# The second phase of a routed expert kernel in a written-out TensorE order

## The chip, the cores and the metric

One core of a Trainium2 chip runs the whole program. The metric is device time in microseconds (us), the median of three runs. Engines: PE is TensorE (matrix products and transposes), DVE is VectorE, ACT is ScalarE, POOL is GpSimd, SP is SyncE, which issues most transfers.

## The reference

The reference computes attention with a threshold, then a dense layer whose hidden value is the largest of three products, then one expert out of eight for each of the 2304 tokens (512 wide, experts 1024 wide):

```python
logits = x @ w_gate + modality_bias[modality_id]
e_idx = np.argmax(logits, axis=1)
...
for e in range(E):
    mask = e_idx == e
    h = np.maximum(x[mask] @ w1[e], 0.0)
    out[mask] = gate_w[mask, None] * (h @ w2[e])
```

Here `x` is the output of the dense layer, and `gate_w` the softmax value of the chosen expert.

## The kernel before

**Arithmetic.** Most products work on operands that are split into a rounded part and the rest (`xh`, `xl`, `wh`, `wl`); one product of the reference is three products on PE, and a `split_out` (ACT rounds, DVE subtracts) stands ahead of each.

**First phase** (`phase1`, `run_tiles`). Attention goes over 128-row tiles: scores (L244), maximum and mask (L259, L254), exponential (L281), transposes (L299, L300), products with the values (L352, in `av`). The dense layer, `moe1`, works on blocks of 256 tokens, nine in all (0 to 8). It is a generator: it issues a few products (L415 for the hidden values, L444 for the output) and yields the time that they stand for, and `fill` runs it between the tiles of attention. A hidden group is 24 products into one PSUM bank; DVE takes maxima from it (L425), ACT rounds (L429), POOL subtracts (L430). Block 6's output, blocks 7 and 8 are left over when attention ends.

**Second phase** (`phase2`). A token's logits (`logits`, `last_logits`: transpose, product with the gate weights, add the bias) lead to the routing. `route_part` finds each token's expert and its place among the tokens of that expert; two small products (L805, L806) count across partitions. `early` does this when blocks 0 to 7 have logits, takes the expert with the most tokens (`estar`), and makes the *early slot*: 384 of its tokens that can be worked on before block 8's tokens are known. `final` does it for all tokens and lays out the other slots of 384 tokens with one expert each; five of them are static. `invert` turns "token goes to place" into "place holds token" by one product for each 128 tokens with the matrix `r_loh` (L860): first the token numbers (`tok`, `gidx`), then a second set for `gate` and `sidx`. A slot is worked through so: POOL gathers its tokens from `xd` in DRAM by `gidx` (L1027), `tokens` transposes and splits them (L1041, `x2h`, `x2l`, 3 sets of 128), `up` makes 8 hidden tiles (12 products of 384 columns each, L1074), `down` adds 72 products of 512 columns (L1095) into three banks, ACT scales them by `gate` (L1099), and POOL scatters the three results to `out` by `sidx` (L1100). `weights` loads and splits an expert's weights, eight pieces of 128x1024, two pieces ahead (L1052, L1054, L1055).

**What sets the order.** The program's text gives a first order, and a planner then moves each engine's instructions by priority and modelled readiness: any PE product may go ahead of an earlier one that is held up. `hot` raises the priority of the routing; `issue_after` holds some work behind an instruction. The order of the end of routing and the early slot stands in `phase2` itself (L560 to L606). Banks: `psM` has two, shared by `moe1`, attention's values and the inversions; in the second phase `moe1` takes `psM` and the two `ph2` banks in turn; three `y2p` and one `pt2` (token transposes) are the rest. Every scatter writes the tensor `out`, so each waits for the one before.

Of the kernel before, what the change touches and what calls it, by code (L numbers as in the profile page):

```python
# [22 lines left out]
E, F2 = 8, 1024  # L23
# [25 lines left out]
class Kern:  # L49
# [5 lines left out]
    def open(self, stack, name, bufs, space=None, side="left"):  # L55
        kw = dict(side=side, reuse_waits="tile")
        if space is not None:
            kw["space"] = space
        return stack.enter_context(self.tc.tile_pool(name=name, bufs=bufs, **kw))

# [177 lines left out]
    def scores(self, lhs):  # L238

        nc = self.nc  # L240
        ps = self.psS.tile([128, 2, 512], F32, name="s")
        for hh in range(2):
            for i, (st, kk) in enumerate(lhs):
                nc.tensor.matmul(ps[:, hh, :288], lhsT=st, rhs=kk[:, hh * 288:hh * 288 + 288],  # L244
                                 start=i == 0, stop=i == len(lhs) - 1)
        return ps
# [47 lines left out]
    def transposes(self, p, outs, p4, c4):  # L294
# [3 lines left out]
        for kt in range(4):  # L298
            nc.tensor.transpose(pt[:, kt, :], p[:, kt * 128:kt * 128 + 128], self.idn)  # L299
        nc.tensor.transpose(p4[:, c4:c4 + 128], p[:, 512:], self.idn)  # L300
# [31 lines left out]
    def av(self, hd, xf):  # L332
# [3 lines left out]
        if hd["na"]:  # L336
# [4 lines left out]
            for kt in range(KT):  # L341
                kk = 128 if kt < 4 else 64
                nc.tensor.matmul(ps[js, :nq], lhsT=f32(hd["vv"][:kk, kt, 0, :]), rhs=f32(hd["pt"][0][:kk, kt, :nq]),  # L343
                                 start=kt == 0, stop=kt == 4)
# [4 lines left out]
        for kt in range(KT):  # L349

            for i, t in enumerate(hd["pt"][:2 if kt < 4 else 1]):
                nc.tensor.matmul(ps[:, :nq], lhsT=vv[:, kt, :, :].rearrange("p a d -> p (a d)"),  # L352
# [48 lines left out]
    def moe1(self, i):  # L401
# [4 lines left out]
        for n0 in range(0, 3 * KF, 2):  # L406
            ps = self.psA()
            for s in range(2):
# [5 lines left out]
                for n, (a, r) in enumerate(ops):  # L414
                    nc.tensor.matmul(ps[:, s * BLK:s * BLK + BLK], lhsT=a, rhs=r, start=n == 0, stop=n == len(ops) - 1)  # L415
                    if n % 4 == 3 and (n < 11 or s == 0):
                        yield 440
            for s in range(2):
# [7 lines left out]
                if m == 2:  # L426
# [5 lines left out]
                    hL.append(l)  # L432
            yield 440
        x1s = []
        for t in range(2):
# [7 lines left out]
            for n, (a, r) in enumerate(ops):  # L443
                nc.tensor.matmul(ps, lhsT=a, rhs=r, start=n == 0, stop=n == len(ops) - 1)  # L444
# [9 lines left out]
        self.x1s = x1s  # L454

    def logits(self, i, x1s):
        nc = self.nc
        for t in range(2):
# [3 lines left out]
            for kc in range(KD):  # L462
                nc.tensor.transpose(pt[:, kc, :], x1[:, kc * 128:kc * 128 + 128], self.idn)
            x1t = self.po.tile([128, KD, 128], F32, name="x1t", bufs=1)
            nc.vector.tensor_copy(x1t, pt)
            yield 440
            pl = self.psL()[:, 0, :]
            for kc in range(KD):
                nc.tensor.matmul(pl[:, :E], lhsT=x1t[:, kc, :], rhs=self.wgs[:, kc, :], start=kc == 0, stop=kc == KD - 1)
            nc.vector.tensor_tensor(self.lg[:, tt, :], pl[:, :E], self.bias[:, tt, :], op=ALU.add)  # L470
            yield 440
        self.logged = i + 1

    def last_logits(self):
        nc = self.nc
        i = NBLK - 1
        xt = []
        for t in range(2):
            pt = self.psL()
            for kc in range(KD):  # L480
                nc.tensor.transpose(pt[:, kc, :], self.x1s[t][:, kc * 128:kc * 128 + 128], self.idn)
# [5 lines left out]
        yield  # L487
        pl = self.psL()
        for t in range(2):
            for kc in range(KD):  # L490
                ins = nc.tensor.matmul(pl[:, t, :E], lhsT=xt[t][:, kc, :], rhs=self.wgs[:, kc, :], start=kc == 0, stop=kc == KD - 1)
        nc.vector.tensor_tensor(self.lg[:, 2 * i:2 * i + 2, :], pl[:, :2, :E], self.bias[:, 2 * i:2 * i + 2, :], op=ALU.add)
        yield ins.ins
# [41 lines left out]
    def phase2(self):  # L535
# [6 lines left out]
        self.nacc = 0  # L542

        def acc():
            self.nacc += 1
            if self.nacc % 2 == 0:
                return self.psM.tile([128, 512], F32, name="m")
            return self.ps2.tile([128, 512], F32, name="ph2", bufs=2)

        self.psA = acc  # L550
        self.route_tiles()
        parts = [self.route_part(0, 14), self.early()]
        need = [14 // 2, 16 // 2]
        self.sidegap = self.tailgap
        while self.fillers or self.side or parts:
            while parts and self.logged >= need[0]:
                self.side.append(parts.pop(0))
                need.pop(0)
            self.fill(1.0)
        t0 = self.eslot  # L560
        hot = lambda: tc.high_priority(offset=self.hot)
        with hot():
            lg = self.last_logits()
            next(lg)
        self.up(t0, 1, (0,))
        with hot():
            ins = next(lg)
        self.p1.close()
        self.pb = opn(ctx, "p2b", 1)
        fin = self.final()  # L570
        with tc.issue_after(ins):
            self.up(t0, 1, (1,))
        with hot():
            ins = next(fin)
        with tc.issue_after(ins):
            self.up(t0, 2)
            self.up(t0, 3)
            self.down(t0, 0)
            self.down(t0, 1)
        with hot():  # L580
            ins = next(fin)
        with tc.issue_after(ins):
            self.down(t0, 2)
        with hot():
            for _ in fin:
                pass
        last = self.estar
        for t in range(NSTAT):
            c = slice(t * G3, t * G3 + G3)
            e = nc.sync.value_load(self.eT[0:1, t * G3:t * G3 + 1], min_val=0, max_val=E - 1)  # L590
            self.slots.append(self.new_slot(self.pa if t % 2 else self.pb, e, e != last, self.gidx[:, c], self.sidx[:, c], self.gate[:, c]))
            last = e
        for t, sl in enumerate(self.slots):
            nxt = self.slots[t + 1] if t < NSTAT else None
            if nxt:
                self.gather(nxt, G3)
            for c in range(NC):
                if t:
                    self.up(sl, c)
                if t and c and nxt:  # L600
                    self.tokens(nxt, c - 1)
            for c in range(NC):
                if t or c > 2:
                    self.down(sl, c)
                if t == 0 and c:
                    self.tokens(nxt, c - 1)  # L606
        n = nc.values_load(self.eT[0:1, NTL:], min_val=NSTAT * G3, max_val=NTL)  # L607
        with tc.For_i(NSTAT * G3, n, G3) as i:
# [9 lines left out]
            sl = self.new_slot(self.pa, e, None, ix[:, :G3], ix[:, G3:], gt)  # L618
# [4 lines left out]
            for c in range(NC):  # L623
                self.up(sl, c)
            for c in range(NC):
                self.down(sl, c)
# [73 lines left out]
    x1s = None  # L700
    conv_rate = (1, 1)
    conv_credit = 0
    tailgap = 3
# [76 lines left out]
    def route_part(self, i0, i1):  # L780
# [23 lines left out]
        pw = self.psM.tile([128, 512], F32, name="m")  # L804
        nc.tensor.matmul(pw[:, :n * E], lhsT=self.below, rhs=ohf, start=True, stop=True)  # L805
        ins = nc.tensor.matmul(pw[:, 256:256 + n * E], lhsT=self.ones, rhs=ohf, start=True, stop=True)  # L806
        self.pw_ins = ins.ins
        ex = t(G, "ex")
        nc.scalar.activation(ex, sh, AF.Exp)
        yield 200  # L810
# [15 lines left out]
        yield 0  # L826
# [11 lines left out]
        yield 0  # L838

    def invert(self, tl, i1, n, name):  # L840
# [12 lines left out]
        for k0, k1 in ((0, 2), (2, NK)):  # L853
# [3 lines left out]
                              self.vals[:, :, k0:k1][:, :i1].rearrange("p t (k o) -> p t k o", o=1).to_broadcast(full), op=ALU.mult)  # L857
            p = self.psM.tile([128, 512], F32, name="m")[:, :(k1 - k0) * n]
            for i in range(i1):
                ins = nc.tensor.matmul(p, lhsT=self.loh[:, i, :], rhs=R[:, i].rearrange("p k s -> p (k s)"),  # L860
                                       start=i == 0, stop=i == i1 - 1)
            tok = t([128, k1 - k0, n], f"tok{k0}")
            v.tensor_copy(tok, p.rearrange("p (k s) -> p k s", s=n))  # L863
            if k0 == 0:
                sc = t([128, n], "sc")
# [291 lines left out]
```

## Time and profile before

| | before |
|---|---|
| median of 3 runs | 931.27 us (930.74 to 932.67) |
| the profiled execution | 935.56 us |
| its span, first to last instruction | 933.8 us |
| mean granted PE clock | 0.966 |
| busy PE / DVE / ACT / POOL | 873.1 / 627.1 / 561.9 / 441.6 us |

The profile is of one execution, whose span is 1.8 us shorter than its time; the median of the runs is 4.3 us below that time. Attention ends at about 609 us, block 8 begins at 645.6 us, the early slot at 687.9, the first static slot at 746.9, and PE's last product starts before 920.9. A product's duration holds its way through the array; what a stream of them costs is the distance between their starts.

### The profile page before, as it was taken

The page shows a single profiled execution, that of the slowest core. Times are in us where ns is not written, and L with a number is a line of the kernel's source. Part 1 is how long each engine was busy: PE and PEld are TensorE (multiplying, and loading weights), DVE is VectorE, ACT ScalarE, POOL GpSimd, SP SyncE. Part 2 cuts the span into 40 slices and gives each one's busy share as a digit, 9 for nine tenths or more (in the row PEclk, how much of TensorE's full clock was granted, in tenths as well). Part 3 has the DMA queues.
Part 4 walks back from the last instruction along what each step waited for, and adds up shares of the span by engine and source line. Part 5 has one row for each costly group of instructions (what it writes and reads, how often), then busy time and mean ns, then how long its engine had stood idle before and what let it go on. Part 6 is the DMA issues. An engine that isn't in the chain of part 4 may idle for free. (4 is left out here: it accounts for less than half of the span.)

```text
span 933.8 us, 16780 instructions
## 1 busy us (share of the span) xinstructions
PE 873.1 (93%) x5598; PEld 775.6 (83%) x5598; DVE 627.1 (67%) x1589; ACT 561.9 (60%) x1167; POOL 441.6 (47%) x635
## 2 busy tenths in 40 slices
PE   7877999999999999999989999999789899999994
PEld 4545876778799899999889999899778698899893
DVE  6998997645588787998797889552525634534430
ACT  4777876756688878889887888611222434444430
POOL 4777877554566667857676765211200212021001
PEclk9998999999999989999989999999789999999998
DMA  6555453322322322322322221000500223411000
GB/s 178 157 160 144 129 150 87 109 63 59 93 57 58 97 71 67 107 67 62 95 77 73 75 69 31 12 13 23 214 2 24 61 64 132 128 57 46 1 34 36
DMA packets 58234, 74.26 MB, mean 80 GB/s; under 512 B 27424, under 2 KB 40480, under 8 KB 58144
## 3 DMA queue, kind: packets, MB, share of 16 engines
q1 hardware_dynamic: 54448, 63.66, 23.5%
q0 software_dynamic: 2880, 9.44, 2.9%
q8 instruction: 46, 0.75, 0.3%
q14 instruction: 44, 0.36, 0.1%
q10 hardware_dynamic: 816, 0.04, 0.1%
HBM read 80.46 MB, written 9.44 MB: 96 GB/s over the span
## 5 line engine op out<-in xcount | busy, mean ns | idle before, releaser
L415 PE MATMUL m<-xh,w 128*128 128x256 f32 x1152 | 235.6, 294 | 4.0 <-DVE e_tok L863 2.2
L415 PEld LDWEIGHTS m<-xh,w 128*128 128x128 f32 x1152 | 190.6, 196 | 7.6 <-DVE e_tok L863 2.4
L415 PE MATMUL m<-xl,w 128*128 128x256 f32 x576 | 167.0, 290 | 1.1 <-POOL xl L379 1.1
L254 DVE SCALAR_TENSOR_TENSOR e<-s,mx,e 128x576 f32<-128x576 f32 x144 | 116.8, 812 | 26.7 <-ACT e L281 23.5
L259 DVE TENSOR_REDUCE mx<-s 128x1 f32<-128x576 f32 x144 | 106.6, 748 | 38.5 <-PE s L244 37.6
L281 ACT ACTIVATE e<-s,mx 128x576 f32<-128x576 f32 x144 | 106.9, 743 | 22.5 <-DVE mx L259 15.5
L415 PEld LDWEIGHTS m<-xl,w 128*128 128x128 f32 x576 | 113.2, 197 | 1.8 <-POOL xl L379 1.3
L1074 PE MATMUL ph<-x2h,w 128*128 128x384 f32 x384 | 107.3, 352 | 1.4 <-ACT x2h L285 1.4
L244 PE MATMUL s<-kk,qh 128*128 128x288 f32 (+1 forms) x272 | 89.5, 359 | 12.4 <-DVE e L254 6.6
L1095 PE MATMUL y2p<-w 128*128 128x512 f32 x432 | 100.8, 391 | 0.0
L216 POOL TENSOR_TENSOR kk<-kr,kk 64x576 fp32r<-64x576 f32 x60 | 88.0, 1467 | 17.7 <-ACT kk L215 8.2
L299 PE MATMUL pt<-idn,e 128*128 128x128 f32 x576 | 91.5, 282 | 4.4 <-ACT th L309 2.6
L1095 PEld LDWEIGHTS y2p<-w 128*128 128x128 f32 x432 | 80.6, 188 | 16.3
L1078 DVE SCALAR_TENSOR_TENSOR w<-ph,w 128x384 fp32r<-128x384 f32 x48 | 26.7, 555 | 90.7 <-ACT w L1077 90.6
L739 DVE TENSOR_TENSOR tl<-pc,th 128x512 fp32r<-128x512 f32 (+1 forms) x104 | 78.3, 760 | 9.7 <-ACT th L311 9.2
L299 PEld LDWEIGHTS pt<-idn,e 128*128 128x128 f32 x576 | 70.5, 145 | 12.2 <-ACT th L309 3.9
L430 POOL TENSOR_TENSOR hl<-hacc,hh 128x256 fp32r<-128x256 f32 x54 | 42.0, 777 | 81.3 <-ACT hh L429 76.8
L267 POOL COPY e<-mx 128x64 f32<-128x64 f32 x144 | 48.6, 342 | 65.8 <-DVE mx L266 51.7
L1077 ACT ACTIVATE w<-ph 128x384 fp32r<-128x384 f32 x48 | 23.6, 492 | 85.7 <-PE ph L1074 84.3
L1074 PEld LDWEIGHTS ph<-x2h,w 128*128 128x128 f32 x384 | 72.8, 195 | 2.6 <-ACT x2h L285 2.1
L343 PE MATMUL m<-th,vv 128*64 128x256 f32 (+3 forms) x240 | 69.1, 427 | 4.2 <-ACT th L322 2.2
L244 PEld LDWEIGHTS s<-kk,qh 128*128 128x128 f32 (+1 forms) x272 | 54.2, 202 | 22.4 <-issue 9.4
(225 smaller groups left out, 2034.0 us busy)
## 6 DMA issues: line engine op xcount, KB each, us to landing
r<-w SPq DMA_DIRECT2D x48, 512.0 KB
kr<-k SPq DMA_DIRECT2D x120, 144.0 KB
tl<-w SPq DMA_DIRECT2D x18, 512.0 KB
qr<-q SPq DMA_DIRECT2D x120, 64.0 KB
vr<-v SPq DMA_DIRECT2D x40, 160.0 KB
xd<-x SPq DMA_DIRECT2D x18, 256.0 KB
vv<-v SPq DMA_DIRECT2D x24, 160.0 KB
tl<-wo SPq DMA_DIRECT2D x6, 512.0 KB
```

What stands on the lines that cost most here:

```text
L216: nc.gpsimd.tensor_tensor(kk[64:128], kr[64:128], f32(kk[64:128]), op=ALU.subtract)
L244: nc.tensor.matmul(ps[:, hh, :288], lhsT=st, rhs=kk[:, hh * 288:hh * 288 + 288], start=i == 0, stop=i == len(lhs) - 1)
L254: self.conv_step(v.scalar_tensor_tensor(e, sv, mx[:, 1:2], e, op0=ALU.is_ge, op1=ALU.mult, accum_out=mx[:, 2:3]))
L259: self.conv_step(v.tensor_reduce(mn[:, 0:1], sn, axis=AX.XY, op=ALU.max, negate=True))
L267: nc.gpsimd.tensor_copy(cur[3][:, S:], mx[:, 4:5].to_broadcast([128, 64]))
L281: nc.scalar.activation(e, sv, AF.Exp, bias=mx[:, 0:1], scale=1.0)
L299: nc.tensor.transpose(pt[:, kt, :], p[:, kt * 128:kt * 128 + 128], self.idn)
L343: nc.tensor.matmul(ps[js, :nq], lhsT=f32(hd["vv"][:kk, kt, 0, :]), rhs=f32(hd["pt"][0][:kk, kt, :nq]), start=kt == 0, stop=kt == 4)
L415: nc.tensor.matmul(ps[:, s * BLK:s * BLK + BLK], lhsT=a, rhs=r, start=n == 0, stop=n == len(ops) - 1)
L739: nc.vector.tensor_tensor(l, src, f32(h), op=ALU.subtract)
L1074: nc.tensor.matmul(ph, lhsT=w[:, cs], rhs=x[:, kc, :], start=n == 0, stop=n == 3 * KD - 1)
L1095: nc.tensor.matmul(sl["y"][g], lhsT=a, rhs=r[:, i, :], start=f == 0 and n == 0, stop=f == KF2 - 1 and n == 2)
```

## The change

- From the end of attention on (`pinned`), every PE product and transpose keeps the order of the program (`mm`, `tp`); the planner no longer moves them, nor past attention's earlier products.
- That order is made by `drive`: a `main` generator (what is left of `moe1`, then slot after slot) yields the time of what it has issued, and side work (logits, `early`, `late_routing`, the next slot's tokens) is put in when the time that it asked for has passed, one piece after the other.
- The early slot is worked as a whole after block 8, beside the end of routing; before, two of its hidden tiles stood ahead of block 8's last groups. Its eight weights are loaded and split during block 8. Its tokens are transposed between products of block 8.
- `invert` for the first static slot is done alone (`g`, 3 places of 39) and its gather issued; then `experts` makes the expert table for slots, not for places; then the inversion of all (`f`).
- `moe1` takes three `ph2` banks in turn, and the token transposes take `psM`.
- The scatters write `dram_disjoint_views` of `out`, one for each set, which are taken as not overlapping.

```diff
+    def mm(self, *args, **kw):
+        return self.pin(self.nc.tensor.matmul(*args, **kw))
...
@@ moe1
+            if i == NBLK - 1 and self.eslot and n0 >= 6:
+                self.weights(n0 // 2)
             yield 440
...
@@ phase2
-        self.psA = acc
+        self.psA = lambda: self.ps2.tile([128, 512], F32, name="ph2", bufs=3)
+        self.outs = dram_disjoint_views(self.out, (NSTAT + 2) * G3)
...
+        self.pinned = True
+        self.slots = []
+        parts = [(lambda: self.logged >= 7, self.route_part(0, 14)), (lambda: self.logged >= 8, self.early()),
+                 (lambda: self.x1i == NBLK - 1, self.late_routing())]
+        self.drive(self.main(), parts)
...
+    def drive(self, main, parts):
+        t = 0.0
+        cur, at = None, 0.0
+        for ns in main:
+            forced = ns is None
+            t += ns or 0.0
+            while True:
+                if cur is None:
+                    if self.side:
+                        cur = self.side.pop(0)
+                    elif parts and parts[0][0]():
+                        cur = parts.pop(0)[1]
+                    else:
+                        break
+                    at = t
+                if t < at and not forced:
+                    break
+                forced = False
+                try:
+                    at = max(t, at) + next(cur)
+                except StopIteration:
+                    cur = None
...
+        for t in range(NSTAT + 1):
+            while len(self.slots) <= t or len(self.slots[t]["done"]) < G3:
+                yield None
+            sl = self.slots[t]
+            if 1 < t < NSTAT:
+                self.side.append(self.next_tokens(self.slots[t + 1]))
+            yield from self.slot(sl)
...
@@ early
+        inv = self.invert(tl, i1, G3, "e", 5000)
+        yield next(inv)
         sc, gidx, _ = next(inv)
...
+        self.gather(sl, G3)
...
         for g in range(G3):
+            yield 3500 if g else 6500
+            self.tokens(sl, g)
...
@@ final
+        first = self.invert(tl, NTT, G3, "g", 10000, rest=False)
+        yield next(first)
+        _, gidx, ins = next(first)
+        with self.tc.issue_after(ins.ins):
+            ins = self.experts(t, nt, st, n1)
+        with self.tc.issue_after(ins.ins):
+            inverse = self.invert(tl, NTT, NTL, "f", 6000)
+            wait = next(inverse)
...
+        self.gather(sl, G3)
+        for g in range(G3):
+            yield 3500 if g else 5000
+            self.tokens(sl, g)
...
@@ tokens
-        pt = self.ps2.tile([128, 4, 128], F32, name="pt2", bufs=1)
+        pt = self.psM.tile([128, 512], F32, name="m").rearrange("p (a b) -> p a b", b=128)
...
@@ down
-                nc.gpsimd.indirect_dma_start(out=self.out, out_offset=bass.IndirectOffsetOnAxis(ap=sl["sidx"][:, g:g + 1], axis=0),
+                nc.gpsimd.indirect_dma_start(out=sl["out"][g], out_offset=bass.IndirectOffsetOnAxis(ap=sl["sidx"][:, g:g + 1], axis=0),
```

What this does to the order, at three places. All PE products of the changed kernel have the lines of `mm` and `tp` (L69, L72).

First PE at the end of attention, before: behind the last transposes (`pt`) stand products of block 6 (`m`, `ph` from `w`), and attention's last values product (`vv`) comes after 20 of them.

```order
L300 MATMUL p_8538<-idn,e 128x128
L299 MATMUL pt<-idn,e 128x128 x4
L444 MATMUL m<-w,hl 128x512
L444 MATMUL m<-w,hh 128x512
L444 MATMUL ph_8646<-w,hh 128x512
...
L444 MATMUL ph_8646<-w,hh 128x512
L463 MATMUL y2p<-idn,x_8643 128x128 x2
L352 MATMUL m<-th,vv 128x320
```

The same place now:

```order
L72 MATMUL pt<-idn,e 128x128 x4
L72 MATMUL p_8538<-idn,e 128x128
L69 MATMUL m<-th,vv 128x320
L69 MATMUL m<-tl,vv 128x320
...
L69 MATMUL m<-th,vv 128x320
L69 MATMUL m<-w,hh 128x512 x2
L69 MATMUL m<-w,hl 128x512
```

The values product now stands right behind the transposes that it needs, and block 6's products behind it.

Second PE at the early slot's tokens (`xg`), before: three sets in a row between block 8 and the slot's first hidden tile.

```order
L444 MATMUL m<-w,hh 128x512
L1041 MATMUL pt_9344<-idn,xg 128x128 x4
L1041 MATMUL pt_9366<-idn,xg 128x128 x4
L1041 MATMUL pt_9386<-idn,xg 128x128 x4
L1074 MATMUL ph_9416<-x2h,w 128x384
```

Now, the first two of the three:

```order
L69 MATMUL ph_9482<-xh,w 128x256 x2
L72 MATMUL m<-idn,xg 128x128 x4
L69 MATMUL ph_9482<-xl,w 128x256
...
L69 MATMUL ph_9528<-xh,w 128x256
L72 MATMUL m<-idn,xg 128x128 x4
L69 MATMUL ph_9571<-w,hh 128x512
```

Each set now stands between products of block 8 (`ph_9482`, `ph_9528`, `ph_9571`); the third stands between `ph_9571` and `ph_9601`.

Third DVE at the early slot's index, before (`e_tok` is what the inversion gives, L1055 the split of a weight):

```order
L863 COPY e_tok_9287<-m 128x6
L866 SCALAR_TENSOR_TENSOR e_sc<-e_tok_9287 128x3
L868 CAST e_gidx<-e_sc 128x3
L1055 TENSOR_TENSOR w<-r_8614,w 128x1024 x3
L863 COPY e_tok_9321<-m 128x12
```

Now:

```order
L874 COPY e_tok_9328<-m 128x6
L1107 TENSOR_TENSOR w<-r_8614,w 128x1024
L876 SCALAR_TENSOR_TENSOR e_gidx<-e_tok_9328 128x3
L880 SCALAR_TENSOR_TENSOR e_sc<-e_tok_9328 128x3
L442 TENSOR_TENSOR hacc<-ph_9298,hacc 128x256
L1107 TENSOR_TENSOR w<-r_8614,w 128x1024
L884 COPY e_tok_9409<-m 128x12
```

The first weight now stands ahead of `e_gidx`, and the other seven between the maxima of block 8 (`hacc`).

## Rows read from the trace of the kernel before

**Rows 1.** What PE waited for from 560 us on: total us, times, longest us

```profile
PE pt L1041 <- DVE x2l L286: 5.7, 4, 1.5
...
PE m L860 <- DVE e_R L856: 3.9, 1, 3.9
...
PE m L415 <- DVE e_tok L863: 2.2, 1, 2.2
...
PE ph L444 <- ACT rs L330: 1.1, 1, 1.1
```

**Rows 2.** Stretches: length, busy PE, PEld, DVE, ACT, POOL, granted clock, DMA share, GB/s

```profile
59.00:60.00 1.00, 1.00 (x4) 0.52 (x4) 1.00 (x3) 1.00 (x4) 0.12 (x2) 0.50 0.82 320
...
664.00:677.00 13.00, 10.85 (x82) 10.55 (x79) 5.30 (x14) 4.08 (x6) 4.43 (x4) 0.66 0.97 377
...
752.00:921.00 169.00, 168.90 (x873) 153.68 (x871) 72.54 (x89) 69.55 (x104) 22.22 (x22) 1.00 0.18 60
```

**Rows 3.** PE in order of time: start, us, line, operation, number [idle before <- whom]

```profile
659.72 0.17 PE L806 MATMUL m<-r_oh,ones 128*128 128x16 bf16 x1
...
663.76 0.59 PE L860 MATMUL m<-e_R,r_loh 128*128 128x6 bf16 x16 [3.87 <-DVE e_R L856]
...
676.39 0.28 PE L415 MATMUL m<-xl,w 128*128 128x256 f32 x1
```

**Rows 4.** PE in order of time, 682 to 755 us

```profile
682.25 0.60 PE L1041 MATMUL pt<-idn,xg 128*128 128x128 f32 x4
...
693.51 0.51 PE L1074 MATMUL ph<-x2h,w 128*128 128x384 f32 x2
...
713.64 0.17 PE L806 MATMUL m<-r_oh,ones 128*128 128x16 bf16 x1
...
732.34 8.41 PE L1095 MATMUL y2p<-w 128*128 128x512 f32 x36
...
740.90 0.66 PE L1041 MATMUL pt<-idn,xg 128*128 128x128 f32 x4
...
751.53 0.51 PE L1074 MATMUL ph<-x2h,w 128*128 128x384 f32 x2
...
753.29 0.60 PE L1041 MATMUL pt<-idn,xg 128*128 128x128 f32 x4
...
753.90 0.34 PE L1074 MATMUL ph<-x2l,w 128*128 128x384 f32 x1
...
754.43 0.34 PE L1074 MATMUL ph<-x2l,w 128*128 128x384 f32 x1
```

**Rows 5.** All engines in order of time, the tail

```profile
918.27 0.69 ACT L1099 ACTIVATE y<-y2p,f_gate 128x512 f32<-128x512 f32 x1 [7.83 <-issue]
...
919.23 0.99 POOL L1100 DMA_INDIRECT out<-y,f_sidx  x1 [25.28 <-ACT y L1099]
...
920.99 0.69 ACT L1099 ACTIVATE y<-y2p,f_gate 128x512 f32<-128x512 f32 x1 [0.67 <-PEq L608]
...
926.16 0.98 POOL L1100 DMA_INDIRECT out<-y,f_sidx  x1 [2.48 <-DMA out<-y,f_sidx]
```

**Rows 6.** All engines in order of time, the end of attention

```profile
601.63 0.59 ACT L304 COPY pc<-pt 128x512 f32<-128x512 f32 x1
...
603.77 0.69 DVE L739 TENSOR_TENSOR tl<-pc,th 128x512 fp32r<-128x512 f32 x1 [1.48 <-ACT th L311]
```

**Rows 7.** PE in order of time, a wait early in attention

```profile
57.86 0.33 PE L300 MATMUL p<-idn,e 128*128 128x128 f32 x1 [2.13 <-POOL e L267]
```

**Rows 8.** DMA issues from 600 us on: number, median us from issue to landing

```profile
xg<-xd,f_gidx POOLq DMA_INDIRECT x15, 3.5
...
xg<-xd,e_gidx POOLq DMA_INDIRECT x3, 7.2
```

**Rows 9.** DVE in order of time

```profile
667.47 2.46 DVE L1055 TENSOR_TENSOR w<-r,w 128x1024 fp32r<-128x1024 f32 x2 [2.51 <-ACT w L1054]
...
723.49 0.88 DVE L851 TENSOR_TENSOR f_toh<-iT,f_tl 128x702 bf16<-128x702 f32 x1
```

More of the change, by code (lines that the diff above doesn't have):

```diff
@@ L59, in open, with pin, tp, lag @@
         return stack.enter_context(self.tc.tile_pool(name=name, bufs=bufs, **kw))
+    pinned = False
+    def pin(self, ins):
+        return self.tc.keep_in_program_order(ins) if self.pinned else ins
+    def mm(self, *args, **kw):
+        return self.pin(self.nc.tensor.matmul(*args, **kw))
+    def tp(self, *args, **kw):
+        return self.pin(self.nc.tensor.transpose(*args, **kw))
+    def lag(self, ns, late):
+        return late if self.pinned else ns
     def setup(self):
@@ L554, in phase2 @@
[L554 to L606, printed above, removed]
+        self.psA = lambda: self.ps2.tile([128, 512], F32, name="ph2", bufs=3)
@@ L622, in phase2, with main, next_tokens, slot @@
                 self.tokens(sl, g)
[L623 to L626, printed above, removed]
+            for x in self.slot(sl):
+                pass
+    def drive(self, main, parts):
[20 more added lines that the diff above has]
+                    cur = None
+    def main(self):
+        while self.fillers:
+            yield from self.fillers.pop(0)
+        for t in range(NSTAT + 1):
[5 more added lines that the diff above has]
+            yield from self.slot(sl)
+    def next_tokens(self, sl):
+        self.gather(sl, G3)
+        for g in range(G3):
+            yield 5000
+            self.tokens(sl, g)
+    def slot(self, sl):
+        for c in range(NC):
+            yield from self.up(sl, c)
+        for c in range(NC):
+            yield from self.down(sl, c)
     def emit_scores(self, heads, tl):
@@ L803, in route_part @@
         ohf = oh.rearrange("p t e -> p (t e)")
[L804 to L807, printed above, removed]
         ex = t(G, "ex")
         nc.scalar.activation(ex, sh, AF.Exp)
-        yield 200
+        yield 2600
+        pw = self.psM.tile([128, 512], F32, name="m")
+        self.mm(pw[:, :n * E], lhsT=self.below, rhs=ohf, start=True, stop=True)
+        self.mm(pw[:, 256:256 + n * E], lhsT=self.ones, rhs=ohf, start=True, stop=True)
         pc = pw[:, 256:256 + n * E].rearrange("p (t e) -> p t e", e=E)
@@ L852, in invert @@
         po = []
-        for k0, k1 in ((0, 2), (2, NK)):
+        for k0, k1 in ((0, 2), (2, NK))[:1 + rest]:
             full = [128, i1, k1 - k0, n]
@@ L938, in unused_away, with late_routing @@
         return sidx
+    def late_routing(self):
+        for gen in (self.last_logits(), self.final()):
+            while True:
+                with self.tc.high_priority(offset=self.hot):
+                    x = next(gen, None)
+                if x is None:
+                    break
+                yield x
     def final(self):
@@ L943, in final @@
         v, bc = nc.vector, self.bc
-        part = self.route_part(2 * (NBLK - 1), NTT)
-        next(part)
-        yield self.pw_ins
-        for _ in part:
-            pass
+        self.p1.close()
+        self.pb = self.open(self.ctx, "p2b", 1)
+        yield from self.route_part(2 * (NBLK - 1), NTT)
         def t(shape, name, dt=F32):
@@ new lines, in final @@
+        last = self.estar
+        for s in range(NSTAT):
+            e = nc.sync.value_load(eT[0:1, s * G3:s * G3 + 1], min_val=0, max_val=E - 1)
+            self.slots.append(self.new_slot(self.pa if s % 2 else self.pb, s + 1, e, e != last, None, None, None))
+            last = e
+        sl = self.slots[1]
+        sl["gidx"] = gidx
+        self.gather(sl, G3)
+        for g in range(G3):
+            yield 3500 if g else 5000
+            self.tokens(sl, g)
+        yield wait
+        sc, self.gidx, _ = next(inverse)
```

159 lines of the change are left out of this document (82 added, 77 removed).

## The prediction

> **What bounds the kernel now.** I began with the list of what TensorE (PE) waited for after 560 us, since the diff rewrites only the second phase. The reader is to see there that the waits are few and sit in three places: the early routing (3.9 and 2.2 us), the transposes of gathered tokens (5.7 us in four waits), and one wait of 1.1 us where the accumulators of the second phase take over the banks of attention [rows 1]. Then the table by stretches: from 752 to 921 us PE is busy for 168.9 of 169 us at a granted clock of 1.00, so a written order can gain nothing there; from 664 to 677 us the clock stands at 0.66 [rows 2]. A wait therefore costs twice, once as idle time and once as products at half clock behind it. PE's own records in order of time give what the three places cost in all [rows 3, 4], and the last scatters show the tail [rows 5]. PE's work is thus the bound; what can be won is idle time, the slow clock behind it, and the tail.
>
> **The change part by part.** *Early routing.* From the second counting product (659.72) to the product that starts at 676.39 pass 16.67 us [rows 3]. In them PE does 48 products of block 8, 0.12 apart at full clock (the 0.18 of 384 columns, below, times 256/384), 5.8 us, and twice 16 inversion products of 0.59 us, 1.2 us. The other 9.7 us are waiting and half clock. In the new order 48 products (5.8 us) stand between the counting products and the first inversion. The chain on VectorE (DVE) before it took 3.9 us; three maxima of block 8 are now mixed into it. I take the wait as gone, with 1 us at most left. Block 8's sums no longer share the two banks of `psM` with the inversion, so the 2.2 us behind `e_tok` go too.
>
> *Early slot's tokens.* From the first transpose at 682.25 to the first of the quick products, at 693.51, pass 11.26 us for three sets of transposes and 17 products [rows 4]. Undisturbed, a set costs 0.43 (753.29 to 753.90 is 0.61, less one product) and a product 0.18 (three in 0.53 from 753.90 to 754.43): 1.3 + 3.0. So 7.0 us go when each set stands between products of block 8, as the new order has it.
>
> *Slot 1's tokens.* The same count from 740.90 to 751.53: 10.63 us for three sets and 14 products, 3.8 undisturbed, so 6.9 us go [rows 4]. This needs `gidx` early. The small inversion stands 60 products (10.6 us) behind the counting ones. The chain between took 9.9 us before (713.64 to 723.49) with two weights and the whole expert table mixed in [rows 4, 9]; the table now comes after it. Behind the inversion 3 products of 0.18 and 21 of the down stage (8.41/36 = 0.23 each) come before the first set, 5.4 us. A gather lands 3.5 us after its issue when nothing else moves [rows 8], so with an issue 1 us after the inversion about 0.9 us are spare, and more for the second and third. The large inversion and its DVE work now lie beside the down stage; slot 1's sums use other banks. Its weights are converted ahead of the second and third tokens on ScalarE (ACT), beside 72 down products, 16.8 us.
>
> *Tail.* The third scatter starts at 926.16, but its row was ready at 920.99 + 0.69 = 921.68. The first started 0.27 after its row (918.96 to 919.23) [rows 5]. With the wait on the scatter before it gone, the third starts at 921.95 and the end comes 4.2 us earlier; what follows it stays. If the views were still taken as one tensor, nothing is gained: 0 to 4.2, and I take 4.2, because in the instruction lists each scatter now waits for its row and its own queue slot alone.
>
> *Added: 18 products* for the lone inversion of slot 1, at 0.59/16 each [rows 3], 0.7 us on PE. The smaller expert table saves DVE time that nobody waited for: nothing.
>
> *Added: order at the end of attention.* Pinned products may not pass attention's last ones any more. Before, 20 products of block 6 stood between the last transposes and the last values product; now nothing does. The chain behind those transposes is a copy at 601.63, a rounding, and the difference that ends at 603.77 + 0.69 = 604.46 [rows 6]: 2.8 us, less 0.6 for a copy of x that stood between them and now comes later (the size of the first copy), so PE stands 2.2 us in place of 1.1 [rows 1]: 1.1 us lost; bounds 0 and 1.7. What is queued behind it on PE is all of block 6's rest and block 7. Does the clock fall? Behind 2.13 us of idle PE at 57.86 it stood at 0.50 from 59 to 60 us [rows 2, 7], so I count a fall. Two falls cost (1 - 0.66) x 13 = 4.4 us in [rows 2]; the shorter here would be some 1.7; bounds 0 and 2.2.
>
> *Moved: the early slot's eight weights* into block 8. Their conversions on ACT and DVE now stand between block 8's maxima, and `e_gidx` stands behind the first of them. That one started 7.8 us behind the counting products (667.47) because the load had not landed [rows 9], so the index is ready at about 9 and the gather issued at 9.4, where PE wants the tokens at 16. Beside the weights a gather took 7.2 us [rows 8], which is 16.6; with later weights out of the way less: 0.4 us, bounds 0 and 3. The Trainium skill, DMA: Bandwidth & Descriptors, SWDGE vs HWDGE vs iDMA, says that each DMA engine takes turns between POOL's and SP's queues; then this gather would land almost as fast as alone and the 0.4 would be 0. The 7.2 us of the row speak against it. Maxima that come late cost nothing while three banks give a group two others' time, 5.8 us.
>
> **The sum.** 9.7 + 7.0 + 6.9 + 4.2 = 27.8, less 0.7 + 1.1 + 1.7 + 0.4 = 3.9: 23.9 us. The profiled execution took 935.56 (span 933.8 and 1.8 around it), which gives 911.7. It was 4.3 over the median of the runs, 931.27; taken from that, **907.4 us**.
>
> **Rivals.** *The waits come back.* The order was written from guessed times. Where PE arrives early it can't turn to anything else, as the old order did. If the early gather or slot 1's is 2 to 3 us late, the clock falls too, and about half of the two token places (7 us) and 3 us of the early routing stay: 917. For it: `e_gidx` behind a weight; against it: 16 us of other work before the tokens.
>
> *The scatters stay in a row*, if the queue keeps the order: 911.6.
>
> *Slower: block 8 is held by its own evictions.* DVE works in order; each weight that has not landed holds the maxima behind it, the three banks fill, and PE waits with the clock falling. Now the loads come at 377 GB/s [rows 2], 1.4 us a weight; eight take 11 us, and block 8 has over 20 left. The point is about 3.5 us a weight (150 GB/s): 28 us in place of 20, and the block's 216 products at half clock, 0.09 more each, 19 us: 27 lost, 3 more than the gain: 934. The Trainium skill, TensorE: Matmul & The Clock Gate, A second HAM failure mode, says that stepping through PSUM banks can leave idle bits between groups that let the clock swing. By this rule block 8 would come near this case without any slow load. Against it, slots 1 to 5 step through two banks from 752 us on at 1.00 [rows 2].
>
> **How the numbers follow.** Forecast 0.71 (902 to 913: with no fall of the clock and no waits 905, with an early routing that gains less 911); waits come back 0.17; scatters in a row 0.05; slower 0.05; no effect 0.02. A measurement here tells 0.2%, 1.9 us, from no change. All but the last two are faster by more: 0.93, 0.02, 0.05. The range runs from 902 to 918, which leaves out the worst of the returned waits and the slow case.
>
> **What would show it.** Right: PE's wait list after 560 us without `e_R`, `e_tok` and `x2l`; granted clock 1.00 from block 7 to the last slot; PE's last product about 20 us earlier; three scatters in the tail 1.3 us apart; a new wait of some 2 us at 600 us with a slow stretch behind it. Wrong: a wait on a gather or on DVE inside block 8, a slow clock between 660 and 750 us, or scatters still 3.5 us apart.

## The result and the profile after

The changed kernel takes **907.63 us** (median of 4 runs, 905.9 to 908.55) beside 931.0 for the kernel before, a ratio of 0.9747 with a 95% interval of 0.9724 to 0.9769. 907.4 was forecast. The profiled execution has a span of 905.9 us.

What PE waited for from 560 us on, now (total us, times, longest; compare [rows 1]):

```profile
PE m L69 <- ACT th L328: 1.4, 1, 1.4
PE m L72 <- DMA xg<-xd,e_gidx: 0.6, 1, 0.6
PE m L69 <- DVE tl L751: 0.3, 1, 0.3
```

`e_R`, `e_tok` and `x2l` are gone. Left are two waits at the end of attention (1.4 + 0.3) and one of 0.6 for the early gather. Stretches of the same profile (columns as in [rows 2]):

```profile
597.67:602.67 5.00, 4.69 (x17) 3.93 (x17) 1.10 (x4) 0.97 (x4) 1.48 (x3) 0.66 0.00 0
...
660.00:670.00 10.00, 10.00 (x109) 9.89 (x106) 8.35 (x16) 7.95 (x11) 5.68 (x5) 1.00 1.02 405
670.00:680.00 10.00, 9.42 (x65) 8.51 (x63) 6.82 (x10) 3.95 (x8) 2.59 (x3) 1.00 0.11 38
...
750.00:890.00 140.00, 140.00 (x724) 127.89 (x723) 58.23 (x71) 57.04 (x83) 19.63 (x19) 1.00 0.18 62
```

The granted clock is 1.00 through both routings and both places of tokens, where it had been 0.66 in the first routing [rows 2]; it falls once, behind the waits of attention's end (0.66 from 597.67 to 602.67). PE in order of time (compare [rows 3, 4]):

```profile
654.01 0.17 PE L69 MATMUL m<-r_oh,ones 128*128 128x16 bf16 x1
...
659.88 0.56 PE L69 MATMUL m<-e_R,r_loh 128*128 128x6 bf16 x16
...
662.29 0.56 PE L69 MATMUL m<-e_R,r_loh 128*128 128x12 bf16 x16
...
670.72 0.63 PE L72 MATMUL m<-idn,xg 128*128 128x128 f32 x4 [0.58 <-DMA xg<-xd,e_gidx]
...
675.00 0.60 PE L72 MATMUL m<-idn,xg 128*128 128x128 f32 x4
...
703.38 0.61 PE L69 MATMUL m<-g_R,r_loh 128*128 128x6 bf16 x18
703.85 0.42 PE L69 MATMUL ph<-x2h,w 128*128 128x384 f32 x1
...
709.25 0.60 PE L72 MATMUL m<-idn,xg 128*128 128x128 f32 x4
...
713.80 0.60 PE L72 MATMUL m<-idn,xg 128*128 128x128 f32 x4
```

From the second counting product to the first inversion pass 5.87 us, which is 48 products at 0.12 us: nothing is lost there. The sets of transposes (four products each) stand 4.3 to 4.6 us apart with other products between.

The early index, on VectorE, and the gather on GpSimd:

```profile
660.47 0.16 DVE L874 COPY e_tok<-m 128x6 f32<-128x6 f32 x1 [0.52 <-PE m L69]
661.78 1.23 DVE L1107 TENSOR_TENSOR w<-r,w 128x1024 fp32r<-128x1024 f32 x1 [1.15 <-ACT w L1106]
662.92 0.15 DVE L876 SCALAR_TENSOR_TENSOR e_gidx<-e_tok 128x3 uint32<-128x3 f32 x1
```

```profile
663.37 1.24 POOL L1078 DMA_INDIRECT xg<-xd,e_gidx  x1 [5.02 <-DVE e_sc L880]
```

The index stands 2.3 us behind its input, because VectorE waits for the first weight and splits it first; the gather issued at 663.37 is used at 670.72. The tail, all engines, and then the DMA issues there (median us from issue to landing):

```profile
894.63 0.99 POOL L1156 DMA_INDIRECT out<-y,f_sidx  x1 [29.62 <-ACT y L1155]
...
896.38 0.69 ACT L1155 ACTIVATE y<-y2p,f_gate 128x512 f32<-128x512 f32 x1 [0.67 <-PEq L572]
897.35 0.98 POOL L1156 DMA_INDIRECT out<-y,f_sidx  x1 [0.38 <-ACTq L572]
```

```profile
out<-y,f_sidx POOLq DMA_INDIRECT x3, 3.6
```

The scatters are issued 1.36 us apart in place of 3.47 [rows 5], but the last lands in 3.6 us, which is also the median of the three, where the same row of the kernel before says 2.7:

```profile
out<-y,f_sidx POOLq DMA_INDIRECT x3, 2.7
```

**Where the time came from.** The last scores product of attention stands ahead of everything that the change touches on PE. Before and after:

```profile
591.66 0.30 PE L244 MATMUL s<-kk,ql 128*128 128x288 f32 x1
```

```profile
587.67 0.30 PE L69 MATMUL s<-kk,ql 128*128 128x288 f32 x1
```

It serves as a marker. From its start to the end of the last product (920.89 and 896.29) pass 329.2 us before and 308.6 after: **20.6 less**, where the terms on PE forecast 9.7 + 7.0 + 6.9 - 0.7 - 1.1 - 1.7 - 0.4 = 19.7. From there to the span's end pass 12.9 and 9.6: **3.3 less**, where 4.2 was forecast. Together 23.9, the forecast sum, because the two misses of 0.9 cancel. The 4.0 us by which the marker itself moved belong to no term: in the profiles of this study it stands anywhere from 585.8 to 594.4, and whole times of one kernel spread by more (the kernel before ran from 928.6 to 941.9 in one comparison). They are close to the 4.3 us by which the profiled execution stood over its median. So the experiments are read first by the time from this marker to the last product, and by the tail.

### The profile page after: what moved, and what is told of

Same layout as the page of the kernel before. It is cut to its first block, busy times and chain, and to the rows that moved or that the text cites. A ratio compares the mean times of both kernels' runs of the same rounds, so it can differ in the third digit from the quotient of the medians.

```text
span 905.9 us, 16816 instructions
## 1 busy us (share of the span) xinstructions
PE 858.6 (95%) x5616; PEld 763.2 (84%) x5616; DVE 627.6 (69%) x1593; ACT 563.1 (62%) x1167; POOL 445.2 (49%) x635
## 4 chain that ended last, share of the span: by engine, by line
PE 59%; issue 18%; DVE 10%; POOL 4%; DMA 4%; ACT 4%; SPq 0%; POOLq 0%; ACTq 0%; DVEq 0%
PE m L69 32%; PE ph L69 9%; PE s L69 8%; PE pt L72 5%; PE y2p L69 2%; DVE e L271 2%; DVE mx L276 2%; POOL out L1156 2%; DVE x L142 1%; PE p L72 1%; POOL xg L1078 1%; DVE x L144 1%; DMA xg<-xd,e_gidx 1%; DVE tl L751 1%; ACT e L298 1%
## 5 line engine op out<-in xcount | busy, mean ns | idle before, releaser
L69 PE MATMUL m<-xh,w 128*128 128x256 f32 x1008 | 202.2, 289 | 1.9 <-ACT hacc L440 0.4
L69 PEld LDWEIGHTS m<-xh,w 128*128 128x128 f32 x1008 | 162.9, 192 | 5.2 <-issue 1.2
L69 PE MATMUL m<-xl,w 128*128 128x256 f32 x504 | 144.4, 287 | 0.0
L69 PE MATMUL m<-th,vv 128*64 128x256 f32 (+5 forms) x440 | 125.7, 370 | 7.3 <-ACT th L328 3.3
L69 PE MATMUL ph<-x2h,w 128*128 128x384 f32 x384 | 103.7, 342 | 0.0
L69 PE MATMUL s<-kk,qh 128*128 128x288 f32 (+1 forms) x272 | 88.8, 357 | 14.2 <-DVE e L271 8.4
L69 PE MATMUL y2p<-w 128*128 128x512 f32 x432 | 100.5, 391 | 0.0
L69 PEld LDWEIGHTS m<-th,vv 128*64 128x64 f32 (+2 forms) x440 | 68.0, 163 | 37.8 <-issue 14.1
L69 PEld LDWEIGHTS m<-xl,w 128*128 128x128 f32 x504 | 96.9, 192 | 0.5 <-issue 0.5
L72 PE MATMUL pt<-idn,e 128*128 128x128 f32 x576 | 91.0, 281 | 6.3 <-ACT th L326 4.3
L69 PEld LDWEIGHTS y2p<-w 128*128 128x128 f32 x432 | 80.7, 188 | 16.3
L72 PEld LDWEIGHTS pt<-idn,e 128*128 128x128 f32 x576 | 69.8, 144 | 14.5 <-ACT th L326 6.1
L447 POOL TENSOR_TENSOR hl<-hacc,hh 128x256 fp32r<-128x256 f32 x54 | 44.3, 821 | 64.8 <-ACT hh L446 60.2
L69 PEld LDWEIGHTS s<-kk,qh 128*128 128x128 f32 (+1 forms) x272 | 53.6, 200 | 24.8 <-DVE e L271 11.5
L69 PEld LDWEIGHTS ph<-x2h,w 128*128 128x128 f32 x384 | 70.2, 188 | 0.2
```

The source lines that it names most:

```text
L69: return self.pin(self.nc.tensor.matmul(*args, **kw))
L72: return self.pin(self.nc.tensor.transpose(*args, **kw))
L447: nc.gpsimd.tensor_tensor(l, acc[f], f32(h), op=ALU.subtract)
```

## The experiments

All but two start from the changed kernel. "PE part" is marker to last product, "tail" the rest of the span, "clock" the granted clock from 10 to 15 us behind the marker, where attention ends.

| run | PE part | PE's waits from 560 us | clock | tail | median us | ratio to before |
|---|---|---|---|---|---|---|
| before | 329.2 | 14.6 | 1.00 | 12.9 | 931.0 | |
| after | 308.6 | 2.3 | 0.66 | 9.6 | 907.6 | 0.9747 (0.9724 to 0.9769) |
| one_out | 307.6 | 2.9 | 1.00 | 13.0 | 911.4 | 0.9745 (0.9703 to 0.9786) |
| before_views | 329.1 | 14.9 | 1.00 | 10.2 | 931.7 | 0.997 (0.9939 to 1.0) |
| attn_fill | 305.8 | 1.2 | 1.00 | 9.8 | 906.3 | 0.9684 (0.9642 to 0.9727) |
| gidx_first | 306.3 | 1.7 | 1.00 | 9.4 | 908.8 | 0.9704 (0.9648 to 0.9759) |
| both_fix | 304.9 | 0.3 | 1.00 | 9.3 | 907.4 | 0.9725 (0.9699 to 0.9751) |
| two_banks | 309.1 | 2.6 | 0.66 | 9.7 | 911.2 | 0.9767 (0.9734 to 0.98) |
| one_inv | 306.7 | 3.3 | 1.00 | 9.5 | 909.6 | 0.9738 (0.9707 to 0.9769) |
| unpinned | 305.3 | 1.1 | 1.00 | 9.2 | 907.5 | 0.972 (0.9688 to 0.9751) |
| unpinned_old_banks | 311.7 | 2.7 | 1.00 | 9.7 | 910.6 | 0.9737 (0.9708 to 0.9765) |
| old_banks | 307.0 | 2.3 | 1.00 | 9.5 | 912.1 | 0.9761 (0.9734 to 0.9789) |
| late_weights | 308.9 | 2.7 | 0.66 | 9.7 | 910.8 | 0.9735 (0.9705 to 0.9765) |
| before_new_banks | 329.8 | 19.6 | 1.00 | 12.9 | 933.2 | 0.9993 (0.997 to 1.0016) |

Each part comes from one profiled execution; parts of like runs agree within 0.3 us once the waits that differ are taken off. The medians were taken at different times, when that of the kernel before was 931.0 to 935.5, so only the ratios compare. For every run that starts from the changed kernel the interval overlaps with that kernel's.

**one_out** and **before_views**, the tail's term.

```diff
-nc.gpsimd.indirect_dma_start(out=sl["out"][g], ...
+nc.gpsimd.indirect_dma_start(out=self.out, ...
```

> The changed kernel, but every scatter writes the whole output tensor again, so that each waits for the one before; no other engine's order differs. Theory (the tail's term holds, and comes from the wait between scatters alone): the last three issues stand 3.5 us apart again in place of 1.36, the last issue comes 4.2 us later, but the last rows land in 2.7 us in place of 3.6, since nothing moves beside them: 3.3 us over the changed kernel's 907.6, so 910.9. Rival 1: the tail is the written order's and stays, 907.6. Rival 2: the early slot's scatters and the gathers behind them are held up too and PE waits for tokens of slot 2: over 913.

In before_views the kernel before gets the views by the inverse edit, one per scatter of a slot.

> The kernel before with the disjoint views alone; PE, VectorE, ScalarE and SyncE have the same order, on GpSimd two gathers move. Theory (the tail's term is independent of the order): 3.3 us under the kernel before, 931.0 - 3.3 = 927.7, with the last three issues 1.4 us apart. Rival: the part needs the rest of the change, within 1 us of 931.

one_out's issues, and how they land:

```profile
895.65 0.98 POOL L1156 DMA_INDIRECT out<-y,f_sidx  x1 [25.30 <-ACT y L1155]
899.15 0.98 POOL L1156 DMA_INDIRECT out<-y,f_sidx  x1 [2.51 <-ACTq L572]
902.65 0.98 POOL L1156 DMA_INDIRECT out<-y,f_sidx  x1 [2.52 <-DMA out<-y,f_sidx]
```

```profile
out<-y,f_sidx POOLq DMA_INDIRECT x3, 2.7
```

Issues 3.5 us apart and a tail of 13.0: 3.4 longer, as the theory said. The median is 911.4 (910.9 expected), but the ratio to the kernel before is the changed kernel's (0.9745 and 0.9747), so the whole time does not show it. The last issue comes 4.2 later behind the last product, and 0.9 comes back because the last rows land faster. In before_views the tail falls from 12.9 to 10.2, 2.7 us, and PE's part stays to 0.1; its rows took longest to land:

```profile
919.37 0.98 POOL L1100 DMA_INDIRECT out<-y,f_sidx  x1 [0.38 <-ACTq L608]
```

```profile
out<-y,f_sidx POOLq DMA_INDIRECT x3, 4.1
```

The part is independent of the order, 2.7 to 3.4 us. The whole time of before_views, 931.7, lies with the rival (within 1 us of 931; 927.7 was the theory), and 1.1 under the 932.8 of the kernel before beside it: the spread of the first phase hides the rest.

**attn_fill**, attention's end.

```diff
         for pend in (self.pend, None):
             for _ in self.finish(heads, pend):
                 pass
+            if pend is not None:
+                self.fill(3600)
```

> The changed kernel with eight products of block 6 written ahead of the last product of values, so that PE has work while the last transposes are copied and split. Theory (attention's end costs what the prediction booked: 1.72 us of waiting and the slow products behind it): no wait of over 0.5 us from 590 to 605 us, granted clock 1.00 there, block 8 starts 2 to 3 us earlier, 905.0. Rival 1: the clock falls at 600 us whatever PE waited, so only 1.2 us are won, 906.4. Rival 2: the copies wait for ScalarE and VectorE, the wait only moves behind, 907.6.

What PE waited for from 560 us on:

```profile
PE m L72 <- DMA xg<-xd,e_gidx: 0.9, 1, 0.9
PE m L69 <- DVE tl L753: 0.3, 1, 0.3
```

The 1.4 us are gone, the clock is 1.00, PE's part is 2.9 shorter, or 3.2 with the gather's waits taken off both. In the profile the theory holds; the median, 906.3, is the number of rival 1, but the slow clock of that rival is not there.

**gidx_first**, the early index. (The first split is written behind the index.)

```diff
+            with self.tc.issue_after(self.egidx.ins) if s == c == k == 0 and self.first_w() else ExitStack():
                 nc.vector.tensor_tensor(wl, raw[:, c, :], f32(wh), op=ALU.subtract)
```

> The changed kernel with one thing moved: on VectorE the early slot's index stands ahead of the first weight's split; all PE work is in the same order. Theory (the 0.58 us that PE waits for the early tokens come from the index, 2.3 us late behind that split): gathers issued at 661.1 in place of 663.4, landing 7.2 us later at 668.3, PE's wait of 0.6 gone, 907.0. Rival: the gather lands only when the weights' loads are through (669 us), however early it is issued: issue to landing 9 us, the wait stays, 907.6.

What PE waited for, and one stretch (columns as above):

```profile
PE m L69 <- ACT th L328: 1.4, 1, 1.4
PE m L69 <- DVE tl L751: 0.3, 1, 0.3
```

```profile
603.19:608.19 5.00, 4.69 (x24) 4.02 (x24) 1.11 (x4) 1.46 (x5) 1.69 (x3) 1.00 0.01 3
```

The wait for the gather is gone, as the theory said; the gather still took 7.3 us. The other 1.8 us are no work of the edit: the same two waits, 1.4 and 0.3, were followed here by a clock of 1.00, and by 0.66 in the changed kernel's profile (both from 10 to 15 us behind the marker). The median, 908.8, does not show the gain (907.0 expected).

**both_fix**, the two edits together.

> The changed kernel with both repairs: eight products of block 6 ahead of the last product of values, and the early slot's index ahead of the first weight's split. Theory: the two add up, last scores to last product 308.6 - 2.9 - 0.9 = 304.8 us in place of 308.6, time 907.6 - 3.8 = 903.8. Rival: the earlier tokens only move the wait to the next set or to slot 1's first tokens: 305.8, 904.8.

PE's part is 304.9, the 304.8 expected, and its only wait is 0.3. The median, 907.4 where 903.8 was expected, does not show it, and the ratio, 0.9725, lies within the changed kernel's interval. Nothing that these runs can tell apart is won in the whole time.

**two_banks**, the accumulators.

```diff
-self.psA = lambda: self.ps2.tile([128, 512], F32, name="ph2", bufs=3)
+self.psA = lambda: self.ps2.tile([128, 512], F32, name="ph2", bufs=2)
```

> The changed kernel with two accumulator banks in place of three; every engine's order is the same. Measured from the last scores product to the last product of all, which takes 308.6 us in the changed kernel's profile. Theory (the prediction's 'maxima that come late cost nothing while three banks give a group two others' time'): with two banks a group has 24 products, 2.9 us, for its two evictions, and in block 8 these stand behind splits of 1.2 to 3.1 us; PE waits for VectorE or ScalarE three to six times between 655 and 685 us, 2 to 5 us in all, the clock may fall behind it: 311 to 315, and the time 910 to 914. Rival 1: two banks are enough, as they are in slots 1 to 5 before: no new wait, 308.6. Rival 2 (stepping through fewer banks keeps the clock steadier): 1 to 2 us under the changed kernel.

```profile
PE ph L69 <- DVE hacc L442: 0.9, 1, 0.9
```

One wait of 0.9 for a maximum, not three to six; it takes the place of the wait for the gather. The third bank is worth under 1 us. The clock in block 8 is 1.00 with two banks as with three.

**one_inv**, the lone inversion. (It is dropped, and slot 1's index is the first part of the large one's.)

```diff
-        first = self.invert(tl, NTT, G3, "g", 10000, rest=False)
...
+        inverse = self.invert(tl, NTT, NTL, "f", 10000)
+        yield next(inverse)
+        sc, self.gidx, ins = next(inverse)
+        gidx = self.gidx[:, :G3]
```

> The changed kernel without the lone inversion of slot 1: slot 1's index is cut from the large inversion, at the same place in PE's order (18 products of 78 columns in place of 6); the 18 products at 724.86 us go. Theory (slot 1's tokens need the small inversion): in VectorE's order the large table and both its factors, 0.88 + 4.62 us in place of 0.20 + 0.27, stand ahead of three evictions of the early slot, and the index and its gather behind them; PE waits 1 to 3 us for evictions or for the first tokens, less 0.8 for the 18 products: 0 to 2 us over the changed kernel, with the waits seen near 702 to 712 us. Rival 1: the three banks take the 5 us up and nothing waits: 0.5 to 0.8 us under the changed kernel. Rival 2: the clock falls behind the wait and half of slot 1's term of 6.9 comes back: 3.5 over.

```profile
702.34 4.62 DVE L865 TENSOR_TENSOR f_R<-f_toh,r_vals 128x1404 bf16<-128x1404 bf16 x2
706.88 1.02 DVE L1128 SCALAR_TENSOR_TENSOR w<-ph,w 128x384 fp32r<-128x384 f32 x2
```

```profile
PE m L72 <- DMA xg<-xd,f_gidx: 0.8, 1, 0.8
```

VectorE does the large factors for 4.62 us with two evictions piled up behind them, and PE waits for none, with three banks. The first tokens come 0.8 late. Even so PE's part is 306.7, or 305.9 with the wait of 0.8 for the early gather taken off, where gidx_first, with the same attention end and no wait for either gather, has 306.3. Rival 1: the lone inversion is worth nothing.

**unpinned** and three runs on banks: what carries the routing and token terms?

```diff
-        self.pinned = True
```

> The changed kernel with the list scheduler in place of the written order in the second phase (the lag of the logits goes back too); three banks, the lone inversion, the early weights and the disjoint views stay. Theory (the gain of the routing and token terms, 9.7 + 7.0 + 6.9, is the written order's): sets of transposes stand in a row again, PE waits 5 us or more between 650 and 750 us and the clock falls: 920 or more. Rival 1: it is the new banks and the early index that gained, and the scheduler finds as good an order: within 2 us of 907.6. Rival 2: half and half, 914.

```profile
PE ph L69 <- ACT rs L347: 1.1, 1, 1.1
```

The theory falls. With the list scheduler (the planner) free again, and with it the old lag of the logits, there is one wait, the 1.1 of [rows 1], and the part is 305.3, shorter than with the pin. The three sets of early tokens even stand nearly in a row, without a wait:

```profile
680.92 1.03 PE L72 MATMUL m<-idn,xg 128*128 128x128 f32 x8
...
683.18 0.60 PE L72 MATMUL m<-idn,xg 128*128 128x128 f32 x4
```

So it could be the banks or the program's order. For the next three the assignment of banks is exchanged, as here or the other way round (`acc` takes a bank of `ph2`, with two, and one of `psM` in turn):

```diff
-self.psA = lambda: self.ps2.tile([128, 512], F32, name="ph2", bufs=3)
+self.psA = acc
-pt = self.psM.tile([128, 512], F32, name="m")
+pt = self.ps2.tile([128, 4, 128], F32, name="pt2", bufs=1)
```

> The kernel before with the changed kernel's banks alone: sums of blocks and slots in three banks of their own, transposes of tokens in the two banks of routing. Its time from the last scores product to the last product of all was 329.2 us. Theory (each of the two sources, order and banks, takes its own waits): the 2.2 us behind e_tok go and the token sets wait about half as long, with less slow clock behind: 322 to 326. Rival 1 (the banks are what the change gained by; the list scheduler finds the rest): 309 or less. Rival 2 (without the new program order the banks do nothing): 329.

Rival 2. The waits only change their names:

```profile
PE m L1033 <- DMA xg<-xd,e_gidx: 9.7, 3, 7.9
PE m L852 <- DVE e_R L848: 2.9, 1, 2.9
PE m L852 <- DVE f_R L848: 2.1, 1, 2.1
```

With the bank free, PE comes to the early tokens sooner and waits for their gather, because the order has nothing else to give it.

> The run without the pinned order, with the banks of the kernel before put back (sums alternate between two banks of their own and the two of routing, tokens in one bank): the new program order, lone inversion and early weights alone. It took 305.3 us from the last scores product to the last product. Theory (both sources count): token sets wait for their one bank and the inversion for block 8's sums, 3 to 8 us with slow clock behind: 308 to 314. Rival 1 (program order is all): 305 to 306.5. Rival 2 (banks are all): 320 or more.

311.7, the theory: 17.5 us shorter than before, by the program's order with the lone inversion and the early weights, and 6.4 longer than with the new banks. PE waits four times more, 1.6 us in all (for ScalarE, GpSimd and VectorE), and the clock falls, which is about (1 - 0.83) x 20 = 3.4 us; the rest is not traced:

```profile
680.00:700.00 20.00, 18.27 (x88) 14.86 (x87) 11.37 (x37) 7.31 (x14) 3.73 (x3) 0.83 0.08 28
```

> The changed kernel, order pinned, with the banks of the kernel before. It took 308.6 us, of which 1.4 the slow clock at 600 us. Theory: as without the pin but worse, since PE can't turn to other work while a bank is held: 311 to 318, with waits at the inversions and the token sets. Rival: 307 to 309, the order spaces the sets so that one bank is enough.

The rival: 307.0 with the old banks, and the waits of the changed kernel to 0.1. With the order pinned no set waits for the one bank.

**late_weights**, the move of the early slot's weights.

```diff
-            if i == NBLK - 1 and self.eslot and n0 >= 6:
-                self.weights(n0 // 2)
```

> The changed kernel with the early slot's weights converted two ahead of their use, as before, in place of within block 8. Theory (the move costs the early gather what the prediction booked, and gains nothing that other engines could not do later): with fewer loads beside it the gather lands in 3.5 to 5 us in place of 7.2 and the wait for it is gone, but the splits now stand in the routing chain behind the second counting products and slot 1's index comes 2 to 4 us later: 308 to 311 us from the last scores product to the last product. Rival 1: the chain has room, and only the gather's wait goes, 306 to 308. Rival 2: PE waits at the early slot's first products for weights, 2 us or more, and the clock falls: 312 or more.

Neither the gain nor the loss. Three of the eight splits still stand where they were, and the other five come from 695.9 us on. SyncE still issues all eight loads at once, ahead of the gather, which takes 7.4 us beside them (PE's wait 1.0), and slot 1's tokens are in time:

```profile
659.70 4.51 SPq L1104 DMA_DIRECT2D r<-w  x8
```

308.9 beside 308.6, both with a fall of the clock behind attention's end:

```profile
600.50:605.50 5.00, 4.69 (x17) 4.16 (x17) 1.10 (x4) 0.60 (x3) 0.88 (x1) 0.66 0.00 0
```

So the earlier conversions are worth nothing that PE's part shows; the loads were not moved by this run.

## Why the prediction was right, and where its reasons were not

**Early routing (9.7) and both token places (7.0 and 6.9): right in their sum.** No wait but 0.6 is left there, and the clock is 1.00. PE's part fell 20.6 for 19.7. With the losses put back as measured (0.6 more waiting and 1.6 of slow clock at attention's end, 0.6 for the gather, 0.5 for the added products) the three places gave 23.9 where 23.6 was booked. No run takes the three apart.

**But what carries them was put wrongly in three places.** "Block 8's sums no longer share the two banks of `psM` with the inversion, so the 2.2 us behind `e_tok` go too": with the old banks under the pinned order they go as well (old_banks), and with the new banks under the old order the loss stays (before_new_banks, 329.8). The banks matter only where the scheduler is free to move the products, 6.4 us. "This needs `gidx` early", by way of the lone inversion: without it PE's part is no longer (one_inv). And the pin is not needed: unpinned is 3.4 us shorter, 1.6 of it the clock at 600 us. What carries 17.5 of the 20.6 us is the order in which the program is written, with the early slot kept whole for the last routing and each step of a chain set behind work that is independent of it. The lone inversion and the early weights stood beside it in that run, and were undone only under the pin, where neither was worth anything. Which part of the order it is was not taken apart further.

**Tail (4.2): mechanism right, size 0.9 too large.** The failed words are "what follows it stays". The last issue did come 4.2 earlier behind the last product (1.06 in place of 5.27), but its rows land in 3.6 us in place of 2.7, so 3.3 remain. That three are in flight does not explain it: slot 4 issues its three 1.36 us apart as well, and they land in 2.7 (first line, median), where the tail's three take 2.7, 4.4 and 3.6:

```profile
out<-y,f_sidx POOLq DMA_INDIRECT x3, 2.7
...
out<-y,f_sidx POOLq DMA_INDIRECT x1, 2.7
out<-y,f_sidx POOLq DMA_INDIRECT x1, 4.4
out<-y,f_sidx POOLq DMA_INDIRECT x1, 3.6
```

What delays the last two stays open.

**Attention's end (1.1 + 1.7): the mechanism right, but the clock's part is a chance, not a rule.** PE stands 1.7 us, where the sum had 2.2, so 0.6 more than the 1.1 of before. The runs that share this wait fall in two groups once PE's other waits from 590 us on are taken off: 308.0, 307.9 and 308.2 where the clock fell (after, late_weights, two_banks), 306.4, 306.4 and 306.3 where it did not (one_out, old_banks, gidx_first). A fall costs 1.6 us, near the 1.7 booked; it came in 3 of the 7 profiles with this wait (one_inv is the seventh), and what decides it no run shows. Without wait and fall it is 304.9 (both_fix, and attn_fill less its 0.9), so the wait costs another 1.5.

**Early gather (0.4): right.** 0.58, by the mechanism named, as gidx_first shows. The Trainium skill, DMA: Bandwidth & Descriptors, SWDGE vs HWDGE vs iDMA, has the DMA engines take turns between the two kinds of queue; by this rule the gather would have landed almost as fast as alone. It took 7.2 us beside the weights before [rows 8], 7.3 in gidx_first and 7.4 in late_weights, against 3.5 for the later slots [rows 8]: for this mix the measurement speaks against the rule's time. That three gathers are issued close together is not the reason, since slot 1's three in the changed kernel, 1.3 to 1.9 us apart, land in 3.7:

```profile
xg<-xd,g_gidx POOLq DMA_INDIRECT x3, 3.7
```

**Added products (0.7): right, a little large.** The 18 take 0.47 us, from 703.38 to 703.85.

**The rivals.** The waits did not come back. Block 8 was not held by its evictions, and with two banks the wait was 0.9 with the clock at 1.00. The Trainium skill, TensorE: Matmul & The Clock Gate, A second HAM failure mode, lets the clock swing where PE steps through PSUM banks; block 8 steps through three, or two, at 1.00 throughout, so nothing of it shows here.

**The profiled execution's 4.3 us over the median** were rightly taken off. That they lie ahead of the marker is likely, not shown: before_views and before_new_banks have the PE part of the kernel before to 0.6 us, with the marker at 589.24 and 593.40.

**Luck.** That the median came within 0.2 us of the forecast owes something to the two misses of 0.9 that cancel, and to a clock that fell in the profiled execution, as booked, but does not fall in all.

## What to carry to other kernels

Write independent work between the steps of a chain, in the program's own order; then neither a pin nor more banks is the main thing, and a pin can cost something at the seam to what stands ahead of it. When a change has several parts, undo each alone: here three (the lone inversion, the earlier conversions, the banks under a pinned order) were worth nothing that these runs show, though each had a good reason. Where whole times spread more than the effect, measure between two instructions that every version has.

## What was not expected of the hardware

The same wait of 1.4 and 0.3 us at the end of attention was followed, from 10 to 15 us behind the marker, by a granted clock of 0.66 in three profiles and of 1.00 in four, with the same products around it in after and gidx_first. Three scatters issued 1.36 us apart landed in 2.7 to 2.8 us each in slots 1 to 4 of the changed kernel, but at the kernel's end the last took 3.2 to 4.1 in the eleven profiles with disjoint views, and 2.7 in the three where each waits for the one before.
